# Softmax bookkeeping of a fused packed-attention and expert kernel: a 33rd column, two steps on GpSimd, a scale on the packed queries, a maximum with its sign turned

## The chip, the cores and the metric

One core of a Trainium2 chip. The metric is device time in microseconds (us) of one execution, as the median of three runs. The engines are TensorE (PE, its weight loads PEld), VectorE (DVE), ScalarE (ACT), GpSimd (POOL) and SyncE (SP, which issues most of the DMAs). Each engine works through its own list of instructions in order.

## The reference

Two attentions in a row, then a layer of eight experts of which each row takes one.

```python
def sm_attn(qq, kk, vv):
    s = scale * np.matmul(qq, kk.transpose(0, 1, 3, 2))   # scale = 1/8
    s = s - np.max(s, axis=-1, keepdims=True)
    a = np.exp(s)
    a = a / (np.sum(a, axis=-1, keepdims=True) + 1e-09)
    return np.matmul(a, vv)
p_packed = sm_attn(p, k, v)          # 32 packed queries against 576 keys
out = sm_attn(q, p_packed, p_packed) # 576 queries against the 32 packed results
...
expert_idx = np.argmax(logits, axis=1)
...
ye = np.maximum(xe @ w1[e], 0.0) @ w2[e]
out[mask] = gate_w[mask, None] * ye
```

Batch 8, heads 8, 576 rows, head size 64; the expert layer has 4608 rows of 512, 8 experts and a hidden size of 1024.

## The kernel before

The first part of the kernel is the attention of eight batches b, the second the expert layer. The attention's steps are written out by hand in the string ORDER, in which each token is one step of one batch: `k`, `v`, `q` issue the loads on SP's queue; `a` and `c` (function `s1`, four heads each) make the scores of the packed queries, their maximum and their exponentials; `r`, `u` and `l` transpose these; `p` (`pv`) multiplies them with v; `b` and `w` (`bd`, `wgp`) lay out the packed result. `S` (`s2`) makes the second attention's scores of two tiles of 128 rows (one tile in the steps ending in 4), `T` (`t2`) transposes their exponentials on TensorE, `O` (`o2`) multiplies and copies out. `E` and `F` are the routing's steps on DVE, `G` the indirect gathers that POOL issues, `P` the layout of the gathered rows, `X` (`scale`) the common scale of all rows. From this program order a planner with costs of its own lays out one list for each engine, so steps that stand behind one another in the program can lie interleaved on an engine.

In `s1` DVE takes the maximum m over 576 scores (L549) and multiplies it by -0.125 (L550); ACT's exponential (L551) takes m as its bias and 0.125 as its scale, and its accumulator gives the sum. When both halves are done, DVE adds 1e-9 to the sums (L560) and takes the reciprocal (L561); `pv` multiplies the reciprocal with a mask (L603) and with the product (L604). The packed queries reach their padded tile by a POOL copy (L493), two per batch.

In `s2` DVE takes the maximum of 32 scores for each of 16 groups (L667), subtracts it (L669) into tile e, ACT takes the exponential in place (L670), DVE sums (L672), adds 1e-9 (L673) and takes the reciprocal (L674), and POOL (for b under VB = 6) or DVE multiplies e by it in place (L676). Tile e has three buffers, and is held from the subtraction to the transposes of `t2` (L685).

POOL also computes the low halves of q (L525, function `split`), on which SP's q loads two buffers later wait, the sums lg of the router's scores (L715, for b under LB = 7), and issues the gathers (L430). In the routing, `of_expert` and `below` share one buffer with the tag "pb", and `places` takes its products mv from a buffer of 1024 elements. In `scale`, DVE spreads the maxima on a diagonal dg (L763), and a matmul with ones (onef, L765) hands every partition all of them.

The expert layer then runs over two groups of row tiles and four chunks of the hidden size: `l1` (L850, L853) and `l2` (L889) on TensorE, and on DVE and ACT the split of each loaded weight tile into a high and a low half (L144, L145). None of its lines is part of the change.

Of the kernel before, what the change touches and what calls it, by code (L numbers as in the profile page):

```python
# [7 lines left out]
F16 = mybir.dt.float16  # L8
F32 = mybir.dt.float32
I32 = mybir.dt.int32  # L10
AF = mybir.ActivationFunctionType
ALU = mybir.AluOpType
AX = mybir.AxisListType
# [3 lines left out]
P = 128  # L17
B, H, S, D = 8, 8, 576, 64
NPACK = 32
# [4 lines left out]
DM = 512  # L24
# [59 lines left out]
def packed_attention_moe(ctx, tc, qT, q1, kT, v4, v1, pT, wg, w1, w2, const, out):  # L84
# [82 lines left out]
    lg = r.tile([P, NT, NE], F32, name="lg")  # L167
    ppm = r.tile([P, B, 2], F32, name="ppm")
    sms = r.tile([P, B, 2], F32, name="sms")
    onef = r.tile([P, P], F32, name="onef")  # L170
    G.memset(onef, 1.0)
    quarter = r.tile([P, 4], F32, name="quarter")
    G.memset(quarter, 0.0)
# [16 lines left out]
    W = 9  # L190
# [108 lines left out]
    def places(k, nt, sf, pool, tag, room=None):  # L299

        a, z = parts[k]
        n = z - a
        inv = pool.tile([P, 4, n], F32, tag=tag, name=f"inv{a}")
        for t0 in range(0, nt, W):
            w = slice(t0, t0 + W)
            if k == 1:
                both = room(t0 // W).bitcast(F16)[:, 0 : 5 * W * n]
                ohs = both[:, 0 : W * n].rearrange("p (w n) -> p w n", n=n)
                mv = both[:, W * n :].rearrange("p (w c n) -> p w c n", c=4, n=n)
            else:  # L310
                ohs = room.tile([P, W, n], F16, tag="ohs", name="ohs", bufs=1)
                mv = room.tile([P, 2 * DM], F16, tag="mv", name="mv", bufs=1)[:, 0 : W * 4 * n]
                mv = mv.rearrange("p (w c n) -> p w c n", c=4, n=n)
            V.tensor_tensor(ohs, bc(cc["number"][:, a:z], [P, W, n], 1), bc(sf[:, w], [P, W, n], 2), op=ALU.is_equal)
            (G if k == 1 and t0 // W in MVG else V).tensor_tensor(
                mv, bc(ohs, [P, W, 4, n], 2), bc(coef[:, w, :], [P, W, 4, n], 3), op=ALU.mult
            )
            if k == 2:
                spread(t0, room)
            yield  # L320
            for t in range(t0, t0 + W):
                T.matmul(inv, ohr[t0][:, t - t0, :], mv[:, t - t0], start=(t == 0), stop=(t == nt - 1))
            yield
        tf = r.tile([P, n], F32, tag="tf", name=f"tf{a}")
        tz = r.tile([P, n], F32, tag="tz", name=f"tz{a}")
        pg = r.tile([P, n], F32, name=f"pg{a}")
        V.tensor_copy(tf, inv[:, 0, :])
        V.scalar_tensor_tensor(tf, inv[:, 1, :], -1.0, tf, op0=ALU.add, op1=ALU.add)
        V.tensor_scalar(gats[k], tf, 0.0, None, op0=ALU.max)
        V.tensor_scalar(tz, tf, 0.0, float(OOB), op0=ALU.is_lt, op1=ALU.mult)  # L330
        V.tensor_tensor(scas[k], tf, tz, op=ALU.add)
        V.tensor_copy(pg, inv[:, 2, :])
        V.tensor_tensor(pg, inv[:, 3, :], pg, op=ALU.add)
        pgs[k] = pg
        yield
# [130 lines left out]
    with ExitStack() as actx:  # L466
# [10 lines left out]
        bds = [one.tile([P, 2, 264], F32, name=f"bd{i}") for i in range(3)]  # L477
        pbs = [one.tile([P, NP, 2 * NPACK], F32, name=f"pb{i}") for i in range(2)]
        aLs = [one.tile([P, 2, P], F32, name=f"aL{i}") for i in range(2)]
        for t in pbs + aLs:  # L480
            G.memset(t, 0.0)

        loaded = {}
        lastld = [None]

        def load_k(b):
            k_s = ld.tile([P, NP, S], F32, tag="k", name=f"k{b}")
            p_s = pbs[b % 2]
            p_r = ld.tile([P, NP, NPACK], F32, tag="p", name=f"p{b}")
            nc.sync.dma_start(p_r, pT[b])  # L490
            for i in range(2):
                r = slice(D * i, D * i + D)
                G.tensor_copy(p_s[r, :, NPACK * i : NPACK * i + NPACK], p_r[r])  # L493
            if b == 0:
                nc.sync.dma_start(k_s[:, 0:2], kT[b][:, 0:2])
                nc.sync.dma_start(k_s[:, 2:4], kT[b][:, 2:4])
            else:
                nc.sync.dma_start(k_s, kT[b])
            loaded[b] = {"k": k_s, "p": p_s}
# [30 lines left out]
        def s1(b, g):  # L530

            k_s, p_s = loaded[b]["k"], loaded[b]["p"]
            if g == 0:

                a = wk.tile([P, 2 * S], F32, tag="a", name=f"a{b}")
                st[b] = {"a": a}
            a, sm = st[b]["a"], sms[:, b, :]
            ps = ps1.tile([P, 2, 512], F32, tag="s1", name="s1")
            for i in range(2):
                for j in range(2):  # L540
                    T.matmul(  # L541
                        ps[64 * j : 64 * j + 64, i, 0:288],
                        p_s[:, 2 * g + j, :],
                        k_s[:, 2 * g + j, 288 * i : 288 * i + 288],
                        start=True,
                        stop=True,
                    )
            m = wk.tile([P, 1], F32, tag="m1", name="m1")
            V.tensor_reduce(m, ps[:, :, 0:288], axis=AX.XY, op=ALU.max)  # L549
            V.tensor_scalar(m, m, -0.125, None, op0=ALU.mult)  # L550
            A.activation(  # L551
                a[:, S * g : S * g + S].rearrange("p (i s) -> p i s", s=288),
                ps[:, :, 0:288],
                AF.Exp,
                bias=m,
                scale=0.125,
                accum_out=sm[:, g : g + 1],
            )
            if g == 1:
                V.tensor_scalar(sm, sm, 1e-9, None, op0=ALU.add)  # L560
                V.reciprocal(sm, sm)  # L561

        def tr(b, g):
# [73 lines left out]
        def s2(b, i):  # L637

            ps = psq.tile([P, 512], F32, tag="s2", name="s2")
            if i < 4:  # L640
                hh = 2 * H
                for n in range(2):
                    for pr in range(NP):
                        for k, (x, y) in enumerate(PRODUCTS):
                            T.matmul(
                                ps[:, 256 * n + 64 * pr : 256 * n + 64 * pr + 64],
                                loaded[b]["q"][i // 2][x][:, pr, P * n : P * n + P],
                                ppTs[b % 3][:, y, pr, :],
                                start=(k == 0),
                                stop=(k == 2),  # L650
                            )
            else:
                hh = H
                for pr in range(NP):
                    for k, (x, y) in enumerate(PRODUCTS):
                        for n in range(2):
                            T.matmul(
                                ps[64 * n : 64 * n + 64, 64 * pr : 64 * pr + 64],
                                loaded[b - 1 + n]["r"][x][:, pr, :],
                                ppTs[(b - 1 + n) % 3][:, y, pr, :],  # L660
                                start=(k == 0),
                                stop=(k == 2),
                            )
                ps = ps[:, 0:256]
            p3 = ps.rearrange("p (h n) -> p h n", n=NPACK)
            m = wk.tile([P, 2 * H], F32, tag="m2", name="m2")[:, 0:hh]
            V.tensor_reduce(m, p3, axis=AX.X, op=ALU.max)  # L667
            e = wk.tile([P, 2 * H, NPACK], F32, tag="e2", name="e2", bufs=3)[:, 0:hh, :]
            V.tensor_tensor(e, p3, m.unsqueeze(2).to_broadcast([P, hh, NPACK]), op=ALU.subtract)  # L669
            last["A"] = A.activation(e, e, AF.Exp, scale=0.125 / SP)  # L670
            sm = wk.tile([P, 2 * H], F32, tag="sm2", name="sm2")[:, 0:hh]
            last["V"] = V.tensor_reduce(sm, e, axis=AX.X, op=ALU.add)  # L672
            V.tensor_scalar(sm, sm, 1e-9, None, op0=ALU.add)  # L673
            V.reciprocal(sm, sm)  # L674
            n, eng = ("V", V) if b >= VB else ("G", G)
            last[n] = eng.tensor_tensor(e, e, sm.unsqueeze(2).to_broadcast([P, hh, NPACK]), op=ALU.mult)  # L676
            return e

        def t2(e):
# [75 lines left out]
        def scale():  # L755

            xm = r.tile([P, 1], F32, name="xm")
            xa = r.tile([P, 1], F32, name="xa")
            V.tensor_tensor(ppm, ppm, sms, op=ALU.mult)
            V.tensor_reduce(xm, ppm, axis=AX.XY, op=ALU.max)  # L760

            dg = r.tile([P, P], F32, name="dg")
            V.tensor_scalar(dg, ident, xm, None, op0=ALU.mult)  # L763
            ps = pst.tile([P, P], F32, tag="tr", name="xmax")
            T.matmul(ps, onef, dg, start=True, stop=True)  # L765
            V.tensor_reduce(xa, ps, axis=AX.X, op=ALU.max)
            pow2(xa, xup, xdn)

# [331 lines left out]
```

## Time and profile before

| | |
|---|---|
| three runs | 618.74, 619.62, 625.78 us; median 619.62 us |
| the profiled execution | 621.44 us, of which its instructions span 619.5 us |
| PE busy | 536.5 us (87% of the span) |
| DVE busy | 469.3 us (76%) |
| ACT busy | 340.7 us (55%) |
| POOL busy | 220.5 us (36%) |

Busy time is the time in which an engine had at least one instruction under way, waits of the instruction for a resource within the engine included. A line such as L673 is a line of the kernel's source. In a row of the timeline the columns are the start, the duration, the engine, line and operation, the tiles written and read, the count, and in brackets the idle time of the engine before it with what ended it. A q behind an engine's name marks its queue: instructions that issue DMAs.

### The profile page before, as it was taken

To read this page: it belongs to the slowest core of one execution; us is meant where nothing else is said; L and a number is where in the kernel's file an instruction comes from. 1 tells how busy PE (TensorE), PEld (TensorE's weight loads), DVE (VectorE), ACT (ScalarE), POOL (GpSimd) and SP (SyncE) were. 2 spreads that over 40 slices of the span, in tenths; PEclk is the share of its full clock that TensorE was granted. 3 is DMA by queue.
4 is the path that set the end of the run, shared out by engine and by line. 5 is a ranking of instruction groups with operands and counts; after the bars stand their busy time and mean duration, and the time that the engine had idled before them with its cause. 6 is when DMAs were issued, how large, how long until landed. Compare 5 with 4: busy or idle time off the path is not lost. (4 is left out here: it accounts for less than half of the span.)

```text
span 619.5 us, 13722 instructions
## 1 busy us (share of the span) xinstructions
PE 536.5 (87%) x4227; PEld 314.3 (51%) x4227; DVE 469.3 (76%) x981; ACT 340.7 (55%) x688; POOL 220.5 (36%) x254
## 2 busy tenths in 40 slices
PE   3899986786768999989999967998999899999990
PEld 1667665565535645634554533455456445445440
DVE  1478995875867998999799849566548988998850
ACT  2568694564447886652772535135877527627400
POOL 2466663521836400330230568662102102201471
PEclk9799997897879999999999998999999999999996
DMA  8987958268748984897697699999859958967751
GB/s 321 397 277 272 394 175 292 85 192 300 245 181 242 245 218 154 180 243 249 158 264 243 182 176 297 281 231 217 191 168 245 274 174 196 273 229 169 138 223 55
DMA packets 132344, 140.13 MB, mean 226 GB/s; under 512 B 96623, under 2 KB 109039, under 8 KB 130352
## 3 DMA queue, kind: packets, MB, share of 16 engines
q1 hardware_dynamic: 116560, 110.62, 66.1%
q0 software_dynamic: 5920, 19.14, 9.8%
q10 hardware_dynamic: 9792, 9.44, 4.5%
q8 instruction: 42, 0.69, 0.5%
q14 instruction: 30, 0.25, 0.1%
HBM read 97.49 MB, written 19.14 MB: 188 GB/s over the span
## 5 line engine op out<-in xcount | busy, mean ns | idle before, releaser
L850 PE MATMUL psa<-w1r,x 128*128 (+1 forms) x656 | 197.0, 383 | 12.0 <-ACT x L713 5.6
L889 PE MATMUL py<-w2r,h 128*128 (+1 forms) x984 | 194.7, 379 | 10.3 <-ACT w2r L144 5.3
L853 PE MATMUL psa<-w1r,x 128*128 (+1 forms) x656 | 163.1, 275 | 0.2 <-DVE x L459 0.2
L863 POOL TENSOR_TENSOR hs<-u,hs 128x256 f16<-128x256 f32 x76 | 66.9, 882 | 243.9 <-DVE hs L862 228.5
L889 PEld LDWEIGHTS <-h 128*128 128x128 f16 (+1 forms) x984 | 87.8, 100 | 114.5 <-issue 13.1
L850 PEld LDWEIGHTS <-x 128*128 128x128 f16 (+1 forms) x656 | 59.7, 101 | 74.7 <-issue 6.3
L898 DVE SCALAR_TENSOR_TENSOR y<-py,gpl,y 128x512 f32<-128x512 f32 x111 | 79.4, 741 | 11.0 <-PE py L889 10.5
L145 DVE SCALAR_TENSOR_TENSOR w2r<-stage,w2r 128x1024 f16<-128x1024 f32 x56 | 74.4, 1328 | 12.4 <-ACT w2r L144 12.2
L855 ACT ACTIVATE u<-psa 128x256 f32<-128x256 f32 x148 | 53.2, 375 | 54.8 <-PE psa L853 44.7
L145 DVE SCALAR_TENSOR_TENSOR w1r<-stage,w1r 128x1024 f16<-128x1024 f32 x56 | 68.1, 1217 | 11.1 <-ACT w1r L144 11.1
L144 ACT ACTIVATE w1r<-stage 128x1024 f16<-128x1024 f32 x56 | 58.0, 1051 | 29.3 <-DMA stage<-w 28.2
L853 PEld LDWEIGHTS <-x 128*128 128x128 f16 (+1 forms) x656 | 59.7, 101 | 15.1 <-issue 7.9
L856 DVE SCALAR_TENSOR_TENSOR u<-psa,u 128x256 f32<-128x256 f32 x148 | 57.7, 413 | 11.7 <-ACT u L855 11.5
L144 ACT ACTIVATE w2r<-stage 128x1024 f16<-128x1024 f32 x56 | 58.5, 1045 | 0.0
L525 POOL TENSOR_TENSOR ql<-q,qh 128x1024 f16<-128x1024 f32 x16 | 34.3, 2143 | 35.2 <-ACT qh L524 34.4
L709 PE MATMUL x<-bd,a2T 128*128 128x264 f32 x128 | 42.2, 457 | 2.6 <-ACT a2T L687 2.4
L900 POOL DMA_INDIRECT out_rows<-y,sca x37 | 37.0, 1000 | 14.4 <-DVE y L898 7.4
L861 ACT ACTIVATE u<-u 128x256 f32<-128x256 f32 x76 | 31.2, 410 | 15.2 <-DVE u L856 14.7
L865 ACT ACTIVATE hs<-u 128x256 f16<-128x256 f32 x72 | 29.6, 412 | 16.4 <-DVE u L856 16.4
L866 DVE SCALAR_TENSOR_TENSOR hs<-u,hs 128x256 f16<-128x256 f32 x72 | 35.2, 490 | 4.4 <-ACT hs L865 4.4
L430 POOL DMA_INDIRECT g<-xd,gat x18 | 23.8, 1323 | 28.3 <-PE psa L853 24.8
L541 PE MATMUL s<-k,pb 128*64 128x288 f32 x128 | 21.9, 468 | 11.4 <-ACT a L551 6.0
(188 smaller groups left out, 680.2 us busy)
## 6 DMA issues: line engine op xcount, KB each, us to landing
stage<-w SPq DMA_DIRECT2D x112, 512.0 KB, 4.6
v<-v SPq DMA_DIRECT2D x8, 1024.0 KB, 8.3
q<-qT SPq DMA_DIRECT2D x16, 512.0 KB, 5.8
k<-kT SPq DMA_DIRECT2D x7, 1152.0 KB, 8.7
xd<-x ACTq DMA_DIRECT2D x22, 256.0 KB, 3.5
xd<-w2r ACTq DMA_DIRECT2D x14, 256.0 KB, 4.2
h<-hs SPq DMA_TRANSPOSE x76, 4.5
k<-kT SPq DMA_DIRECT2D x2, 576.0 KB
```

The lines of the kernel that those rows point to most:

```text
L144: A.activation(hi, src, AF.Copy, scale=SW)
L145: V.scalar_tensor_tensor(lo, src, SW, hi, op0=ALU.mult, op1=ALU.subtract)
L709: T.matmul(ps, aT[:, 2 * n + g, :], bds[b % 3][:, g, :], start=True, stop=True)
L850: T.matmul(ps[c], x[:, 0, k, c], w, start=(k == 0), stop=False, **kw)
L853: last["T"] = T.matmul(ps[c, 0:FC], x[:, 1, k, c], w, start=False, stop=(k == 3), **kw)
L855: A.activation(u, ps[:, FC:], AF.Copy, scale=SH)
L856: V.scalar_tensor_tensor(u, ps[:, 0:FC], SH, u, op0=ALU.mult, op1=ALU.add)
L863: last["G"] = G.tensor_tensor(hs[:, 1], u, hs[:, 0], op=ALU.subtract)
L866: last["V"] = V.scalar_tensor_tensor(hs[:, 1], u, 0.0, hs[:, 0], op0=ALU.max, op1=ALU.subtract)
L889: last["T"] = T.matmul(ps[c], h[:, hp, f, c], w, start=(n == 0), stop=(n == 5), **kw)
L898: last["V"] = V.scalar_tensor_tensor(y, ps, at(gpls, j), y, op0=ALU.mult, op1=ALU.add)
L900: i = G.indirect_dma_start(out, bass.IndirectOffsetOnAxis(ap=at(scas, j), axis=0), yt.pop(j), None, bounds_check=NT * P - 1, oob_is_err=False,
```

## The change

Four edits, and three that only make room in memory:

- `s2`: the exponentials go into one of two lasting tiles of 16 groups of 33 columns, whose 33rd column holds 1e-9 from the start. The sum runs over 33 columns, and DVE's addition L673 goes away. The multiplication by the reciprocal no longer works in place: it reads this tile and writes tile e, which now has two buffers in place of three.
- `s1`: the addition of 1e-9 to the two sums goes from DVE to POOL; DVE's reciprocal stays behind it.
- `load_k`: POOL's copy of the packed queries becomes a multiplication by 0.125.
- `s1`: the exponential no longer scales, and DVE's L550 goes away: the maximum is taken with its sign turned in the reduction itself.
- Memory: onef shrinks from 128 columns to one that the matmul in `scale` reads 128 times over, dg shares the tag "pb", and the first stage's mv shrinks to what it uses.

```diff
-    onef = r.tile([P, P], F32, name="onef")
+    onef = r.tile([P, 1], F32, name="onef")
...
-                mv = room.tile([P, 2 * DM], F16, tag="mv", name="mv", bufs=1)[:, 0 : W * 4 * n]
+                mv = room.tile([P, 2 * DM if k else W * 4 * n], F16, tag="mv", name="mv", bufs=1)[:, 0 : W * 4 * n]
...
+        e1s = [one.tile([P, 2 * H, NPACK + 1], F32, name=f"e1{i}") for i in range(2)]
+        ne = [0]
...
+        for t in e1s:
+            G.memset(t[:, :, NPACK : NPACK + 1], 1e-9)
...
-                G.tensor_copy(p_s[r, :, NPACK * i : NPACK * i + NPACK], p_r[r])
+                G.tensor_scalar(p_s[r, :, NPACK * i : NPACK * i + NPACK], p_r[r], 0.125, None, op0=ALU.mult)
...
-            V.tensor_reduce(m, ps[:, :, 0:288], axis=AX.XY, op=ALU.max)
-            V.tensor_scalar(m, m, -0.125, None, op0=ALU.mult)
+            V.tensor_reduce(m, ps[:, :, 0:288], axis=AX.XY, op=ALU.max, negate=True)
...
-                scale=0.125,
...
             if g == 1:
-                V.tensor_scalar(sm, sm, 1e-9, None, op0=ALU.add)
+                G.tensor_scalar(sm, sm, 1e-9, None, op0=ALU.add)
                 V.reciprocal(sm, sm)
...
-            e = wk.tile([P, 2 * H, NPACK], F32, tag="e2", name="e2", bufs=3)[:, 0:hh, :]
-            V.tensor_tensor(e, p3, m.unsqueeze(2).to_broadcast([P, hh, NPACK]), op=ALU.subtract)
-            last["A"] = A.activation(e, e, AF.Exp, scale=0.125 / SP)
+            e1 = e1s[ne[0] % 2][:, 0:hh, :]
+            ne[0] += 1
+            V.tensor_tensor(e1[:, :, 0:NPACK], p3, m.unsqueeze(2).to_broadcast([P, hh, NPACK]), op=ALU.subtract)
+            last["A"] = A.activation(e1[:, :, 0:NPACK], e1[:, :, 0:NPACK], AF.Exp, scale=0.125 / SP)
...
-            last["V"] = V.tensor_reduce(sm, e, axis=AX.X, op=ALU.add)
-            V.tensor_scalar(sm, sm, 1e-9, None, op0=ALU.add)
+            last["V"] = V.tensor_reduce(sm, e1, axis=AX.X, op=ALU.add)
             V.reciprocal(sm, sm)
             n, eng = ("V", V) if b >= VB else ("G", G)
-            last[n] = eng.tensor_tensor(e, e, sm.unsqueeze(2).to_broadcast([P, hh, NPACK]), op=ALU.mult)
+            e = wk.tile([P, 2 * H, NPACK], F32, tag="e2", name="e2", bufs=2)[:, 0:hh, :]
+            last[n] = eng.tensor_tensor(
+                e, e1[:, :, 0:NPACK], sm.unsqueeze(2).to_broadcast([P, hh, NPACK]), op=ALU.mult
+            )
             return e
...
-            dg = r.tile([P, P], F32, name="dg")
+            dg = r.tile([P, P], F32, tag="pb", name="dg")
...
-            T.matmul(ps, onef, dg, start=True, stop=True)
+            T.matmul(ps, onef.to_broadcast([P, P]), dg, start=True, stop=True)
```

## Rows read from the trace of the kernel before

**Rows 1.** Busy time by stretch: microseconds, engines PE to POOL, TensorE clock, DMA share, GB/s

```profile
0.00:28.00 28.00, 15.70 (x162) 10.13 (x162) 6.89 (x22) 9.12 (x18) 9.40 (x29) 0.88 0.95 358
28.00:96.00 68.00, 62.91 (x1003) 46.33 (x1002) 59.48 (x140) 51.61 (x115) 42.91 (x51) 0.98 0.76 278
96.00:134.00 38.00, 28.66 (x431) 22.20 (x430) 26.17 (x94) 19.15 (x43) 13.37 (x19) 0.86 0.50 174
134.00:182.00 48.00, 31.50 (x248) 22.34 (x242) 31.34 (x119) 21.06 (x46) 17.60 (x19) 0.82 0.78 259
182.00:606.00 424.00, 397.78 (x2393) 213.27 (x2393) 345.40 (x609) 239.79 (x468) 135.58 (x138) 0.99 0.86 216
```

**Rows 2.** Groups by line, 0 to 310 us: busy us, mean ns, idle before

```profile
L672 DVE TENSOR_REDUCE sm<-e 128x16 f32<-128x512 f32 (+1 forms) x20 | 12.3, 620 | 3.2 <-ACT e L670 3.1
L673 DVE TENSOR_SCALAR sm<-sm 128x16 f32<-128x16 f32 (+1 forms) x20 | 6.4, 324 | 0.1
L560 DVE TENSOR_SCALAR sms<-sms 128x2 f32<-128x2 f32 x8 | 4.8, 596 | 2.7 <-ACT a L551 2.7
L493 POOL COPY pb<-p 64x128 f32<-64x128 f32 x16 | 4.6, 289 | 8.1 <-DMA p<-pT 7.6
...
L715 POOL TENSOR_TENSOR lg<-w2r 128x8 f32<-128x8 f32 x14 | 2.8, 205 | 7.5 <-ACT w2r L713 7.5
L550 DVE TENSOR_SCALAR m<-m 128x1 f32<-128x1 f32 x16 | 2.3, 146 | 0.2
```

**Rows 3.** DVE's busy time in L673 alone, by stretch

```profile
28.00:96.00 68.00, 4.93 (x12) 0.98 0.76 278
96.00:134.00 38.00, 0.81 (x5) 0.86 0.50 174
134.00:182.00 48.00, 0.62 (x3) 0.82 0.78 259
```

**Rows 4.** DVE's busy time in L560 alone

```profile
28.00:96.00 68.00, 4.27 (x5) 0.98 0.76 278
```

**Rows 5.** DVE's busy time in L550 alone

```profile
28.00:96.00 68.00, 1.58 (x11) 0.98 0.76 278
```

**Rows 6.** Timeline, one pack's sums beside POOL's split of q

```profile
35.59 2.13 POOL L525 TENSOR_TENSOR ql<-q,qh 128x1024 f16<-128x1024 f32 x1 [1.05 <-ACT qh L524]
...
36.55 1.20 DVE L560 TENSOR_SCALAR sms<-sms 128x2 f32<-128x2 f32 x1 [0.30 <-ACT a L551]
...
37.67 1.05 POOL L676 TENSOR_TENSOR e<-e,sm 128x512 f32<-128x512 f32 x1
...
37.78 0.17 DVE L561 RECIPROCAL sms<-sms 128x2 f32<-128x2 f32 x1
```

**Rows 7.** Timeline, a sum of s2 beside POOL's split, and POOL beside DVE

```profile
91.23 2.33 POOL L525 TENSOR_TENSOR ql<-q,qh 128x1024 f16<-128x1024 f32 x1 [1.60 <-ACT qh L524]
...
91.48 2.11 DVE L673 TENSOR_SCALAR sm<-sm 128x16 f32<-128x16 f32 x1
...
93.62 0.25 DVE L674 RECIPROCAL sm<-sm 128x16 f32<-128x16 f32 x1
...
95.01 1.21 DVE L145 SCALAR_TENSOR_TENSOR w1r<-stage,w1r 128x1024 f16<-128x1024 f32 x1
95.02 1.72 POOL L525 TENSOR_TENSOR rl<-r,rh 128x256 f16<-128x256 f32 x1
```

**Rows 8.** Timeline, POOL's products of s2 and DVE's next subtraction but one

```profile
80.92 1.62 POOL L676 TENSOR_TENSOR e<-e,sm 128x512 f32<-128x512 f32 x2 [0.18 <-DVE sm L674]
...
81.48 0.69 DVE L669 TENSOR_TENSOR e<-s,m 128x512 f32<-128x512 f32 x1
```

**Rows 9.** Timeline, the attention's two long stalls on ACT and TensorE

```profile
104.13 0.38 ACT L623 ACTIVATE ppT<-bd 128x256 f16<-128x256 f32 x1 [4.11 <-DMA v<-v]
...
172.85 0.38 ACT L713 COPY x<-x 128x264 f32<-128x264 f32 x1 [6.88 <-POOL lg L715]
...
174.89 0.59 PE L850 MATMUL psa<-w1r,x 128*128 x1 [5.57 <-ACT x L713]
```

## The prediction, made before the change was run

> **What bounds the kernel now.** I first cut the span by stages with the view of busy time by stretch [rows 1]. From 182 us on the expert layer holds TensorE: 397.78 of 424 us busy at a granted clock of 0.99. No line of the change lies there. What the change can move is the time at which that stage begins. Ahead of it stand four stretches. Up to 28 us the transfers set the pace (DMA share 0.95, DVE busy for 6.89 us). From 28 to 96 us two engines are nearly full: TensorE with 62.91 of 68 us, DVE with 59.48. From 96 to 182 us none is full (TensorE 60.2 of 86, DVE 57.5): the attention's last batches run as a chain of short steps, with stalls such as the 4.11 us in which ACT waits for the load of v, and the 6.88 us in which it waits for POOL's sums of the router's scores behind the gathers, after which TensorE's first expert tile comes 5.57 us late [rows 9].
>
> Second, I asked what DVE's 59.48 us are made of. L673 adds a constant to 16 numbers in each partition; over all stretches it has a mean of 324 ns, L560 (two numbers) one of 596 ns, while L550 (one number) takes 146 ns [rows 2]. The timeline says why. L560 at 36.55 us lasts 1.20 us and ends 0.03 us behind POOL's split of q; L673 at 91.48 us lasts 2.11 us and ends 0.03 us behind another one [rows 6, 7]. These instructions are held by POOL, and the hold counts as busy. It goes the other way too: POOL's split of 256 columns took 1.72 us beside DVE's L145 [rows 7]. Undisturbed, L673 takes some 0.16 us (0.81 us for five from 96 to 134 us [rows 3]), so its 12 in this stretch are 4.93 us, of which 12 x 0.16 = 1.9 us is their own work and 3.0 us hold; L560's five are 4.27 us, some 3.4 us of it hold [rows 4]; three of the five look like the one in [rows 6].
>
> The Trainium skill's page SBUF — State Buffer, section "Who interferes with whom", says that DVE's copies and tensor_scalar in a two-port mode, and DVE instructions with two SBUF inputs, take a pair of ports that GpSimd also needs, whoever comes first holding it for the whole instruction. The two timelines agree [rows 6, 7]. By the same rule the addition moved to POOL would be held whenever one of DVE's two-input instructions runs.
>
> **The change part by part.** I sum against the profiled execution, 621.44 us (span 619.5 us).
>
> *L673 goes, 20 times.* Between 28 and 96 us that is 4.93 us of DVE's time [rows 3]. Against it each sum runs over 528 in place of 512 numbers, 16/512 of 620 ns = 19 ns, or 0.4 us for all 20 [rows 2]. A hold isn't wholly gained: if DVE's next two-input instruction falls into the same split, it is held in its place. I take 3.5 us. From 96 to 182 us the eight others are 1.43 us [rows 3], in a chain where a step saved may count or may only lengthen another wait: 0 to 1.4 us, I take 0.5.
>
> *L550 goes, 16 times.* Eleven lie between 28 and 96 us, 1.58 us [rows 5]; starts of neighbouring short instructions lie closer than their durations, so I take 1.0. It also shortens the way from the scores to the exponential by some 0.15 us in each `s1`; up to 28 us that is covered by transfers, and I take 0.3 there. The turned sign within the reduction is not in the trace; its nearest row without one is the same reduction, and I take no cost, with 16 x 0.15 = 2.3 us as the other end, which would cancel this part.
>
> *L560 moves to POOL, 8 times.* DVE loses 4.27 us between 28 and 96 us [rows 4], but L561 now waits for POOL, and behind L561 on DVE stand L603 and the next maxima. Where POOL is idle the addition costs what its smallest arithmetic costs, 0.2 us (128x8, L715 [rows 2]). Where a split runs, the addition waits for its end, just as the held L560 did: in [rows 6] it could start at 37.72 us, and L561 comes at about 38.0 us in place of 37.78, or past 38.9 us if POOL's product of 1.05 us goes first. DVE gains only if the planner put other work ahead of L561. On POOL the addition waits in order for ACT's accumulator, and behind it stand the split of q, on which SP's next q load waits, and the products on which TensorE's transposes wait; POOL has 25 us of idle time in the 68 [rows 1]. Ends: a gain of 4.3 us, a loss of 8 (next part). I take a gain of 0.5.
>
> The Trainium skill's page GPSIMD Engine Reference, section "Engine selection", advises VectorE and not GpSimd for elementwise work on a tile. Here the nearest rows differ by 0.04 us (0.205 us against L673's undisturbed 0.16), so by size alone it changes nothing; the wait does.
>
> *Buffers.* Before, a subtraction needed the transposes of three steps earlier; now it needs the product of two steps earlier, and the product needs the transposes of two steps earlier. I went through ORDER for each step: the closest case is the subtraction at 81.48 us, which needs the product of two steps before, ended by about 82.0 us in [rows 8]. That is a wait of 0.5 us for DVE, less the 0.2 us by which that product can come earlier without L673. In all other steps the older product or transpose has ended in time. Cost 0.3 us.
>
> *The packed queries' scale.* POOL's 16 copies of 289 ns become multiplications of the same size [rows 2]. They lie right behind their load and a batch or more ahead of their use; if a multiplication took twice as long it would be 4.6 us of POOL's time, hidden by its idle time. Cost nothing; uncovered only for the first batch, 0.3 us at most. The memory edits and the ones read as a broadcast touch one matmul, and dg is read before anything else takes its buffer, since DVE itself waits for that matmul: nothing.
>
> *The sum.* DVE gains 3.5 + 1.0 + 0.5 - 0.3 - 0.2 (12 longer sums) = 4.5 us between 28 and 96 us. TensorE has only 68 - 62.91 = 5.1 us of idle time there [rows 1], so even if DVE alone caused all of it, no more than about that can come out. With 0.3 us before and 0.5 us behind, 5.3 us; of it I count 5, since the later stalls for transfers partly swallow it. The expert layer shifts as a whole. 621.44 - 5 = 616.4 us for the profiled execution; the median of the runs lies 1.8 us under it, so 614.6, and I say 615.
>
> **The rivals.**
>
> *It is swallowed* (about 619.5 us). TensorE's 62.91 us of 68 speak for it: if its weight loads and matmuls were the true limit, DVE's time would turn into waiting. So does the 4.11 us stall behind v's load [rows 9]. Against it speaks that v's load is itself issued when a product of the attention frees its buffer, so it would move along.
>
> *Slower: L561 blocks DVE* (about 624 us). In the three packs where L560 is long today, POOL has a split of 2.13 us under way and a smaller split (a quarter of its columns, so some 0.5 us) or a product (1.05 us) behind it [rows 6]. If the planner puts the addition behind all of these, it ends up to 2.13 + 0.5 + 1.05 + 0.2 = 3.9 us behind the accumulator, against some 1.3 us today (4.27 us less two undisturbed ones, by three): 2.6 us more in three packs, 7.8 us, and with the five others 8 us. Less the 4 us that L673 and L550 give, 4 us more than now: 619.62 + 4 = 624. From the point at which DVE's new waits at L561 exceed about 4.5 us, the change loses. Against it: a planner that sees POOL's queue can set L561 later.
>
> *More than the sum* (about 607 us). All that goes from DVE is 6.4 + 4.8 + 2.3 = 13.5 us [rows 2]; if all of it counted, 619.62 - 13.5 = 606. A smaller piece with the same result would be another order on POOL near 170 us, which takes away part of the 6.88 us stall [rows 9]. TensorE's small idle time between 28 and 96 us speaks against the first, and nothing in the change aims at the second, though the planner lays all lists out anew.
>
> *The change doesn't do what it says:* the new tile's rows of 33 columns could be slower to write or read for ACT, DVE or POOL. The trace has no such form; 20 steps with 0.1 us each on four instructions would be 8 us of engine time, partly hidden, and this ends near the swallowed case.
>
> **How the numbers follow.** Forecast 615 us (611 to 618): chance 0.44. Swallowed, the slow rows of 33 with it: 0.23. Slower: 0.18. More: 0.15. Two per cent, about what a measurement of this kernel can tell from no change (its three runs lie 7 us apart), is 12.4 us: 607.2 and 632.0. Half of the case "more" lies under the first; of "slower" a quarter over the second, with two or three stalls of the kind of [rows 9] added. So 0.09 faster, 0.05 slower, 0.86 within. For 8 in 10 I leave out the lower half of "more" and the upper part of "slower": 605 to 627 us.
>
> **What would show it.** Right: DVE's sum of the attention shorter by some 10 us of busy time, no DVE instruction of two numbers held for over a microsecond, TensorE's L850 of [rows 9] some 5 us earlier than 174.89 us, the rest shifted. Wrong: DVE idle ahead of L561 with POOL as the releaser, above 4 us in total; a first expert tile at the same time or later; a reduction L549 that takes longer than before; or an expert layer that itself got longer or shorter, which no step here explains.

## The result, and the profile after

The changed kernel takes 618.51 us (median of 20 runs), the kernel before 624.71 us in 20 runs beside it: a ratio of 0.9872, with a 95% interval of 0.9834 to 0.991. The medians lie 6.2 us apart; the ratio, which leaves out the runs more than 1.5% above the fastest of their kernel (ten of the changed kernel's 20), makes it 8 us (624.71 times 0.0128), or 1.3%, and within the two per cent of the prediction. The profiles show less, spans of 619.5 and 619.8 us before and 614.9 us now: both of before are of executions (621.44 and 621.7 us) some 3 us under its median. The first profile of the changed kernel fell on an execution of 621.07 us, slower than its median; the rows below are from a second one, of 616.92 us.

Busy time by stretch of the changed kernel, the stretches of [rows 1] (columns: PE, PEld, DVE, ACT, POOL, TensorE's granted clock, DMA share, GB/s):

```profile
0.00:28.00 28.00, 19.22 (x286) 12.20 (x286) 9.07 (x23) 12.40 (x24) 13.45 (x34) 1.00 0.94 364
28.00:96.00 68.00, 62.23 (x899) 45.65 (x898) 51.24 (x112) 49.63 (x115) 46.04 (x59) 0.96 0.79 292
96.00:134.00 38.00, 30.01 (x429) 23.65 (x429) 29.22 (x90) 20.80 (x44) 13.33 (x20) 0.81 0.60 207
134.00:182.00 48.00, 35.22 (x282) 24.61 (x281) 37.65 (x126) 26.10 (x57) 26.53 (x24) 0.92 0.81 270
182.00:606.00 424.00, 391.32 (x2333) 209.60 (x2333) 338.05 (x588) 232.22 (x450) 125.26 (x131) 0.97 0.86 210
```

Two things stand out against [rows 1]. DVE is 8.2 us less busy between 28 and 96 us. And the first stretch, in which I had expected 0.3 us, holds 286 matmuls in place of 162: the attention gets ahead before 28 us. From 134 to 182 us all engines do more, since the expert layer begins sooner.

Groups of the same kernel by line, from 0 to 310 us (busy us, mean ns, idle before), which answer to [rows 2]:

```profile
L676 DVE TENSOR_REDUCE sm<-e 128x16 f32<-128x528 f32 (+1 forms) x20 | 12.7, 635 | 0.3 <-ACT e L674 0.3
...
L554 DVE TENSOR_REDUCE m<-s 128x1 f32<-128x576 f32 x16 | 12.0, 752 | 11.9 <-PE s L546 11.6 <-PE wgp L635 0.3
...
L498 POOL TENSOR_SCALAR pb<-p 64x128 f32<-64x128 f32 x16 | 8.4, 528 | 10.9 <-DMA p<-pT 7.7 <-PE s L546 2.6
...
L606 DVE TENSOR_TENSOR ms<-sms,quarter 128x8 f32<-128x8 f32 x8 | 5.0, 623 | 0.2
...
L563 POOL TENSOR_SCALAR sms<-sms 128x2 f32<-128x2 f32 x8 | 1.7, 214 | 5.2 <-ACT a L555 3.8 <-ACT sh L234 1.1
...
L564 DVE RECIPROCAL sms<-sms 128x2 f32<-128x2 f32 x8 | 1.3, 163 | 5.1 <-POOL sms L563 5.1
```

The sum over 33 columns costs 15 ns more, against the 19 forecast, and the reduction with its sign turned 752 ns, as without (751 ns). POOL's addition takes 214 ns. The reciprocal now waits 5.1 us in all for it: over 4 us of this the prediction had named as a sign of its being wrong, and the time fell all the same. L606, the product behind it, has a mean of 623 ns where its undisturbed time is 166 ns: two of its eight are held, by 1.8 us each. Before, three were held, by 0.6 to 0.8 us:

```profile
L603 DVE TENSOR_TENSOR ms<-sms,quarter 128x8 f32<-128x8 f32 x8 | 3.3, 413 | 0.3
```

One of the two:

```profile
41.37 0.21 POOL L563 TENSOR_SCALAR sms<-sms 128x2 f32<-128x2 f32 x1
...
41.61 0.17 DVE L564 RECIPROCAL sms<-sms 128x2 f32<-128x2 f32 x1 [0.89 <-POOL sms L563]
...
41.66 2.13 POOL L530 TENSOR_TENSOR ql<-q,qh 128x1024 f16<-128x1024 f32 x1
41.81 2.00 DVE L606 TENSOR_TENSOR ms<-sms,quarter 128x8 f32<-128x8 f32 x1
```

In this timeline of the changed kernel POOL's next split begins 0.05 us behind the reciprocal, and the next DVE instruction with two inputs is held for 1.8 us. So a hold taken from L560 can pass on to its neighbour. In sum a part of it does: L606 is busy for 1.7 us more than L603 was, and the 4.8 us of L560 are gone from DVE.

### The profile page after: what moved, and what is told of

Same layout as the page of the kernel before. It is cut to its first block, busy times and chain, and to the rows that moved or that the text cites. A ratio compares the mean times of both kernels' runs of the same rounds, so it can differ in the third digit from the quotient of the medians.

```text
span 618.9 us, 13689 instructions
## 1 busy us (share of the span) xinstructions
PE 539.1 (87%) x4227; PEld 314.8 (51%) x4227; DVE 464.4 (75%) x937; ACT 341.7 (55%) x688; POOL 225.5 (36%) x264
## 4 chain that ended last, share of the span: by engine, by line
PE 42%; DMA 6%; DVE 5%; ACT 3%; issue 2%; POOL 0%; POOLq 0%; ACTq 0%; DVEq 0%
PE py L895 27%; PE psa L856 10%; PE psa L859 5%; DMA stage<-w 3%; DVE w2r L145 2%; ACT w2r L144 2%; DMA g<-xd,gat 2%; DMA x<-xs 2%; DVE u L862 1%; DVE hs L872 1%; ACT hs L871 0%; ACT u L867 0%; DVE xs L449 0%; DVE hs L868 0%; ACT u L861 0%
## 5 line engine op out<-in xcount | busy, mean ns | idle before, releaser
L895 PE MATMUL py<-w2r,h 128*128 (+1 forms) x984 | 198.7, 384 | 17.8 <-ACT w2r L144 14.4
L145 DVE SCALAR_TENSOR_TENSOR w2r<-stage,w2r 128x1024 f16<-128x1024 f32 x56 | 74.8, 1336 | 12.1 <-ACT w2r L144 11.9
L145 DVE SCALAR_TENSOR_TENSOR w1r<-stage,w1r 128x1024 f16<-128x1024 f32 x56 | 68.8, 1228 | 11.6 <-ACT w1r L144 11.6
L144 ACT ACTIVATE w1r<-stage 128x1024 f16<-128x1024 f32 x56 | 58.1, 1052 | 28.8 <-DMA stage<-w 26.8
L862 DVE SCALAR_TENSOR_TENSOR u<-psa,u 128x256 f32<-128x256 f32 x148 | 57.9, 413 | 13.6 <-ACT u L861 13.4
L530 POOL TENSOR_TENSOR ql<-q,qh 128x1024 f16<-128x1024 f32 x16 | 35.1, 2196 | 14.8 <-ACT qh L529 11.7
L872 DVE SCALAR_TENSOR_TENSOR hs<-u,hs 128x256 f16<-128x256 f32 x72 | 36.6, 508 | 4.3 <-ACT hs L871 4.0
L430 POOL DMA_INDIRECT g<-xd,gat x18 | 22.4, 1245 | 28.3 <-PE psa L859 24.2
L546 PE MATMUL s<-k,pb 128*64 128x288 f32 x128 | 22.4, 465 | 11.5 <-ACT a L555 6.2
```

Of the source, the lines that this page charges most:

```text
L144: A.activation(hi, src, AF.Copy, scale=SW)
L145: V.scalar_tensor_tensor(lo, src, SW, hi, op0=ALU.mult, op1=ALU.subtract)
L862: V.scalar_tensor_tensor(u, ps[:, 0:FC], SH, u, op0=ALU.mult, op1=ALU.add)
L872: last["V"] = V.scalar_tensor_tensor(hs[:, 1], u, 0.0, hs[:, 0], op0=ALU.max, op1=ALU.subtract)
L895: last["T"] = T.matmul(ps[c], h[:, hp, f, c], w, start=(n == 0), stop=(n == 5), **kw)
```

## The experiments

All were timed in five rounds beside the kernel before. For each I read when certain steps begin: the product of the second and of the sixth batch (DVE's reduction behind `pv`), the first gather on POOL, and the first `l2` product on TensorE, with the span of the same profile. The expectations number their theories: 1, the work and the holds that DVE lost are the gain; 2, the lists as the planner newly laid them out; 3, the move of L560 alone; 4, L550's place between the maximum and the exponential of `s1`. The runs were spread over three chips, on which the kernel before had medians from 622.63 to 627.83 us: times are compared as ratios, and a span is that of one execution.

| kernel | 2nd batch | 6th batch | first gather | first l2 | span | ratio (interval) |
|---|---|---|---|---|---|---|
| before | 31.6 | 96.3 | 154.2 | 214.5 | 619.5 | |
| before again | 31.8 | 96.5 | 151.3 | 211.2 | 619.8 | 1.004 (1.000 to 1.008) |
| changed, again | 27.3 | 92.8 | 146.6 | 206.0 | 614.9 | 0.987 (0.981 to 0.993) |
| column alone | 31.8 | 91.3 | 147.5 | 206.5 | 611.2 | 0.989 (0.984 to 0.994) |
| maximum's sign alone | 26.4 | 90.6 | 151.7 | 211.7 | 617.7 | 0.992 (0.988 to 0.996) |
| POOL's addition alone | 32.5 | 96.9 | 150.6 | 210.7 | 619.1 | 0.988 (0.979 to 0.997) |
| changed without maximum | 34.0 | 94.0 | 145.3 | 206.3 | 613.8 | 0.991 (0.985 to 0.996) |
| changed without column | 26.9 | 89.8 | 148.1 | 207.3 | 624.6 | 0.986 (0.972 to 1.001) |
| changed without POOL's addition | 28.8 | 92.3 | 148.3 | 206.2 | 617.8 | 0.996 (0.992 to 1.001) |
| no additions at all | 27.2 | 90.9 | 147.7 | 207.2 | 620.2 | 0.989 (0.980 to 0.999) |
| L673 back, as scalar | 27.2 | 91.4 | 140.4 | 199.4 | 606.3 | 0.977 (0.973 to 0.982) |
| L673 back, as reduction | 26.5 | 90.8 | 143.3 | 204.4 | 614.0 | 0.992 (0.987 to 0.997) |
| before, a multiplication more | 31.6 | 102.0 | 156.8 | 217.3 | 624.1 | 1.013 (1.007 to 1.020) |

**The changed kernel again.** No edit.

> The changed kernel once more, for a second profile. All theories: 0.987 of the kernel before, as measured (0.983 to 0.991). Theory 1 (what DVE lost was real work and holds, so the attention ends earlier): the last product of the first attention (matmuls pv) ends about 8 us before 133.9 us, the last copy of the second one about 12 us before 174.5 us, as in the first profile. Theory 2 (the planner's new lists removed single stalls by chance): the same times, but the gain sits in one or two places, the stall of 4.1 us behind v's load and that of 6.9 us behind the gathers. Open besides: the wait of 10.9 us that TensorE had near 380 us in the first profile. If it belongs to the changed kernel it comes again; if it is a matter of one execution it is some 3 us, as in the kernel before.

Measured: 0.9874. The steps come within 2 us of the first profile's, and the long wait of TensorE near 380 us came again (8.6 us after 10.9 us, below), so it belongs to this kernel.

**The kernel before again.** No edit.

> The kernel before, unchanged, as a second profile of it and as the measure of what a ratio means here. All theories: ratio 1.000 (0.995 to 1.005), the holds of DVE behind POOL in the same places as in its first profile (some 12 us of them between 28 and 96 us), the last copy of the second attention near 174.5 us, the first l2 product near 214.5 us.

Measured: 1.004, with an interval that just takes in 1. The holds lie in the same places, and the lists of the engines are the same, instruction by instruction. Between two profiles of one program the first gather differs by 2.9 us: less than that is read from no row of the table behind the sixth batch.

**Each part alone.** The column:

```diff
+            e1 = e1s[ne[0] % 2][:, 0:hh, :]
...
-            V.tensor_scalar(sm, sm, 1e-9, None, op0=ALU.add)
```

> The kernel before with the 33rd column alone (two lasting tiles of 33 columns, product not in place, L673 gone, the memory edits); L550 and L560 stay on DVE. Theory 1: this is the largest part, 4 to 5 us faster, ratio 0.992 to 0.994. Theory 2 (plan and stalls): no order can be told, anything from 0.98 to 1.01. Theory 3 (the move of L560 to POOL is the gain, since it held DVE for 3.4 us): nothing, 0.999 to 1.001.

The maximum:

```diff
-            V.tensor_reduce(m, ps[:, :, 0:288], axis=AX.XY, op=ALU.max)
-            V.tensor_scalar(m, m, -0.125, None, op0=ALU.mult)
+            V.tensor_reduce(m, ps[:, :, 0:288], axis=AX.XY, op=ALU.max, negate=True)
```

> The kernel before with the scale on the packed queries and the sign turned in the reduction alone: L550 gone, POOL's copies are multiplications. Theory 1: 1 to 1.5 us faster, ratio 0.998. The reduction with the turned sign takes the same 0.75 us. POOL's multiplication showed 0.53 us against the copy's 0.29 in the changed kernel; hidden by POOL's idle time. If that were not hidden: up to 3 us slower, 1.005.

POOL's addition:

```diff
-                V.tensor_scalar(sm, sm, 1e-9, None, op0=ALU.add)
+                G.tensor_scalar(sm, sm, 1e-9, None, op0=ALU.add)
```

> The kernel before with only the addition L560 moved to POOL. Theory 1: 0 to 1 us faster, ratio 0.998 to 1.000, since the addition waits for the same split of q as the held instruction did. Theory 3: 3 to 8 us faster, 0.987 to 0.995. The rival of the prediction (DVE's reciprocal blocked): 4 to 8 us slower, 1.006 to 1.013, with DVE idle ahead of the reciprocal and POOL as the releaser.

Measured: 0.9893, 0.9919 and 0.9882. Each part alone gives about two thirds of the whole or more; together they give hardly more than one. No theory that adds terms foretold that. The table shows that they get there by different ways. Against the first profile of before, the sign alone is 5.2 us ahead at the second batch and 5.7 us at the sixth, and then loses it (2.5 us ahead at the first gather, and 0.4 us behind the second profile's). The column alone is level at the second batch and 5.0 us ahead at the sixth. POOL's addition alone is 0.4 to 0.9 us behind both profiles at these two, and behind them all its steps and its span come within 0.7 us of the second profile of before. So the move itself shows no gain in the trace, and nothing there answers to its ratio of 0.988, whose interval reaches 0.997. In it the rival of the prediction can be seen at work once:

```profile
61.52 2.13 POOL L525 TENSOR_TENSOR ql<-q,qh 128x1024 f16<-128x1024 f32 x1
63.60 1.05 POOL L676 TENSOR_TENSOR e<-e,sm 128x512 f32<-128x512 f32 x1
64.61 0.67 POOL L525 TENSOR_TENSOR rl<-r,rh 128x256 f16<-128x256 f32 x1
65.36 0.21 POOL L560 TENSOR_SCALAR sms<-sms 128x2 f32<-128x2 f32 x1
```

```profile
65.61 0.17 DVE L561 RECIPROCAL sms<-sms 128x2 f32<-128x2 f32 x1 [1.42 <-POOL sms L560]
```

The addition stood behind a split, a product and a smaller split, as priced, and DVE waited 1.42 us; in the other places it did not stand so far back (5.5 us of such waits in all).

**Each part taken out of the changed kernel.** Edits: the lines above, turned back one part at a time.

> The changed kernel without the scale on the packed queries and the turned sign (L550 back on DVE, POOL copies): column and POOL's addition alone. Theory 4, formed from the runs so far: L550 stands between the maximum and the exponential of s1, whose scores have one PSUM buffer, so the way from one s1 to the next passes through it and through whatever DVE has in front of it; with the turned sign the exponential starts 0.03 us behind the maximum, without it 0.8 to 1.5 us behind in the first four steps. Then the second batch's product (ppm, L600 of before) comes near 31.7 us, as in the kernel before, and not near 27.3 us as in the changed one, and the whole is 2 to 5 us slower than the changed kernel, ratio 0.991 to 0.995. Theory 2 (only the lists as a whole matter): product near either, ratio anywhere from 0.975 to 1.01.

> The changed kernel without the 33rd column: turned sign and POOL's addition alone; L673 on DVE, three buffers of e, product in place. Theory 4: second batch's product near 27.3 us; ratio 0.985 to 0.992. Theory 1 (L673 is the largest part): half of the gain or less is left, 0.994 to 0.997, with L673 held for 1 to 2 us in some places. Theory 2: no telling.

> The changed kernel with L560's addition back on DVE: column and turned sign alone. Theory 4: second batch's product near 27.3 us, ratio 0.983 to 0.990, and no wait of DVE's reciprocal for POOL (1.99 us at 95.8 us in the changed kernel). If the addition on POOL is a gain of its own: 2 to 4 us slower than the changed kernel, 0.991 to 0.994. If that wait costs: 1 to 3 us faster, 0.982 to 0.985.

Measured: 0.9906, 0.9864 (with an interval up to 1.001) and 0.996. The second batch obeys theory 4 in every kernel of the table: with the sign turned in the reduction it comes at 26.4 to 28.8 us, with L550 in place at 31.6 to 34.0 us. The total does not: without the column the ratio is no worse, and without POOL's addition it is worse, though the 1.99 us wait is gone; its interval, 0.992 to 1.001, touches that of the changed kernel's second timing (0.981 to 0.993).

**L673 back on DVE.** First as it was, then a reduction over one column in its place.

```diff
-            last["V"] = V.tensor_reduce(sm, e1, axis=AX.X, op=ALU.add)
+            last["V"] = V.tensor_reduce(sm, e1[:, :, 0:NPACK], axis=AX.X, op=ALU.add)
+            V.tensor_scalar(sm, sm, 1e-9, None, op0=ALU.add)
```

> The changed kernel with L673's addition put back on DVE (sum over 32 columns, then the addition as a tensor_scalar on the 16 sums); the new tiles, the move to POOL and the sign stay. Theory 1: 3 to 5 us slower than the changed kernel, ratio to the kernel before 0.993 to 0.996; some of these 20 instructions are held for 1 to 2 us. Theory 2: no telling order, about 0.99. If the buffers of the changed kernel are the gain: 0.987, no loss.

```diff
-            last["V"] = V.tensor_reduce(sm, e1, axis=AX.X, op=ALU.add)
+            last["V"] = V.tensor_reduce(sn, e1, axis=AX.X, op=ALU.add)
+            V.tensor_reduce(sm, sn.unsqueeze(2), axis=AX.X, op=ALU.add)
```

> As the run before, but in the addition's place stands a reduction over one column on DVE (20 of them, each copying the 16 sums): the same count of DVE instructions in the same place, of a kind whose instances never lasted longer in the trace of before (sums over 32 columns, maxima and reciprocals show no such spread). Theory 1, with the hold as the main part: 1 to 2 us slower than the changed kernel, ratio 0.989 to 0.991, 2 to 3 us better than with the tensor_scalar. If the instruction's own work or place in the chain is the price: as the run before.

Measured: 0.9773 and 0.9921. With 20 instructions more, one of them held for 1.6 us, the first is the fastest kernel of the study (607.6 us, median), 1% under the changed one. Its interval, 0.973 to 0.982, is clear of that of the changed kernel's 20 runs and just touches that of its second timing. The second, whose added reductions are held nowhere (0.28 us at most), is slower than the first by 1.5%, the reverse of what was expected.

```profile
L677 DVE TENSOR_SCALAR sm<-sm 128x16 f32<-128x16 f32 (+1 forms) x20 | 5.6, 282 | 0.1
```

```profile
102.14 1.76 DVE L677 TENSOR_SCALAR sm<-sm 128x16 f32<-128x16 f32 x1
```

So the time that L673 takes, holds included, is not what the total follows; theory 1 falls here. Twelve of the 20 additions lie ahead of the sixth batch, which comes at 91.4 us with them and at 92.8 us without.

**A second multiplication in the kernel before.**

```diff
-            V.tensor_scalar(m, m, -0.125, None, op0=ALU.mult)
+            V.tensor_scalar(m, m, -0.25, None, op0=ALU.mult)
+            V.tensor_scalar(m, m, 0.5, None, op0=ALU.mult)
```

> The kernel before with one DVE instruction more in each s1: the factor -0.125 is put on in two steps, -0.25 and 0.5. It adds work and lets the planner lay out its lists anew. Theory 1 (work taken from DVE is the gain): 1 to 2.5 us slower, ratio 1.002 to 1.004. Theory 2 (the lists of the kernel before happen to be poor, so that any edit that lays them out anew gains): faster, 0.988 to 0.996, with fewer holds than 12 us between 28 and 96 us though DVE has more to do.

Measured: 1.0134, some 8 us slower for 2.3 us of DVE's work. Not any new layout gains, then, so theory 2 in its plain form falls too. DVE's busy time between 28 and 96 us fell to 48.09 us in it, from 59.48, and the kernel is the slowest: that number says little of how far the attention has come.

**No additions.** The kernel before with the turned sign, and both lines that add 1e-9 left out.

> The kernel before with the turned sign, and with both additions of 1e-9 left out (a sum of exponentials that holds the maximum's own is at least 1, where 1e-9 is under half a unit of float32); e in place with three buffers, no 33rd column, nothing moved to POOL. Least work of all versions. Theory 1 and theory 4: as fast as the changed kernel or faster, 0.980 to 0.988. Theory 2 (lists): anywhere from 0.975 to 1.0, not ordered by work. A version that beats both kernels, if theory 4 holds and the waits for POOL and the holds are what is left.

Measured: 0.9892. The version with the least work is not the fastest.

## Why the prediction was right, and which of its terms were not

**The whole.** Forecast were 5 us less; 5 (spans of the second profiles), 6 (medians) and 8 (ratio) were measured, and the attention ends sooner and the expert layer shifts, as named. The 618.51 us themselves lie just above the 611 to 618 us of this case, because the kernel before, counted from 619.62 us, came out at 624.71 us. In all 14 profiles, the changed kernel's first one included, the first `l2` product comes 58 to 61 us behind the first gather, and the span ends 405 to 417 us behind that product. This last length differs by 3.6 us between the two profiles of the kernel before and by 5.9 us between those of the changed one, so no part of it is put down to the change.

The place of the gain is not the one forecast. Of the 5.3 us, 4.5 were to come between 28 and 96 us and 0.3 ahead of them. The changed kernel is 4.3 us ahead of the kernel before at the second batch and 3.5 us at the sixth: it has its lead by about 30 us, and nothing is added up to the sixth batch. That the sum came out right is in good part luck: one of its terms was mis-sized by some 4 us, and its largest one isn't seen.

For the kernel before, for the changed one and for the version with L673 back, TensorE's products with the second weights (last figures: first and last start):

```profile
L889 PE MATMUL py<-w2r,h x984: 376/379/631, 211.2 to 605.2; 128*128 x159, 128*64 128x512 f16 x38
```

```profile
L895 PE MATMUL py<-w2r,h x984: 376/379/631, 206.0 to 599.9; 128*128 x159, 128*64 128x512 f16 x38
```

```profile
L896 PE MATMUL py<-w2r,h x984: 376/379/632, 199.4 to 591.4; 128*128 x159, 128*64 128x512 f16 x38
```

**L673 (3.5 us, the largest term): not borne out.** With it back, the sixth batch came no later and the kernel was the fastest. The column alone does gain 5.0 us by the sixth batch, but as the version with L673 back is as far by then (91.4 us), that gain isn't shown to be L673's. My own caution, that a hold passes on to the next instruction with two inputs, is what the trace shows once (L606 above). It goes both ways: here, in the changed kernel, DVE's L145 is held by POOL's product until 91.75 us, and POOL's next split then takes 3.11 us:

```profile
90.70 1.05 POOL L680 TENSOR_TENSOR e<-e,sm 128x512 f32<-128x512 f32 x1 [2.75 <-ACT w1r L144]
...
91.01 1.82 DVE L145 SCALAR_TENSOR_TENSOR w1r<-stage,w1r 128x1024 f16<-128x1024 f32 x1
...
91.71 3.11 POOL L530 TENSOR_TENSOR ql<-q,qh 128x1024 f16<-128x1024 f32 x1
```

**L550 (1.3 us with the first stretch): mis-sized, and its cover misread.** I wrote that transfers cover the first 28 us. But the scores of `s1` have one PSUM buffer, so its steps stand in a chain: matmul, maximum, L550, exponential, next matmul. ACT's rows in the second profile of before and in the changed kernel:

```profile
8.96 1.28 ACT L551 ACT_TABLE_LOAD   x1 [8.96 <-DVE m L550]
10.26 0.74 ACT L551 ACTIVATE a<-s,m 128x576 f32<-128x576 f32 x1
```

```profile
0.73 1.28 ACT L555 ACT_TABLE_LOAD   x1 [0.73 <-PEq L1085]
8.88 0.74 ACT L555 ACTIVATE a<-s,m 128x576 f32<-128x576 f32 x1 [6.87 <-DVE m L554]
```

The third step, in the same two profiles:

```profile
18.19 0.76 DVE L549 TENSOR_REDUCE m<-s 128x1 f32<-128x576 f32 x1 [1.25 <-PE s L541]
19.83 0.50 DVE L748 SCALAR_TENSOR_TENSOR wgp<-wgs,wgp 128x32 f16<-128x32 f32 x1 [0.89 <-ACT wgp L747]
20.25 0.14 DVE L550 TENSOR_SCALAR m<-m 128x1 f32<-128x1 f32 x1
```

```profile
20.49 0.74 ACT L551 ACTIVATE a<-s,m 128x576 f32<-128x576 f32 x1 [0.69 <-DVE m L550]
```

```profile
18.16 0.76 DVE L554 TENSOR_REDUCE m<-s 128x1 f32<-128x576 f32 x1 [2.84 <-PE s L546]
```

```profile
18.95 0.74 ACT L555 ACTIVATE a<-s,m 128x576 f32<-128x576 f32 x1 [0.36 <-DVE m L554]
```

From the end of the maximum to the start of the exponential the first four steps took 1.56, 0.76, 1.54 and 1.41 us before, 5.3 us in all; with the turned sign they take 0.03 or 0.04 us each. 1.3 us of it is the load of ACT's table, which waited with the first exponential and now runs at the start. The rest is the multiplication itself, and what stands between: in the second and the fourth step a copy that ACT has ahead of the exponential, in the third a DVE instruction that waits for ACT. That answers to the 3 to 5 us by which the kernels with this part are ahead of the kernel before at the second batch, against the 0.3 us forecast. In the whole this part alone gave 0.8%.

**L560 (0.5 us): no gain is seen.** The addition waits for the same splits as L560 did. Before, L560 and L603 were busy for 4.8 and 3.3 us and DVE stood 2.7 us ahead of L560, 10.8 us in all; now it is 5.0 us for L606 and 5.1 us of waiting for POOL, 10.1 us: 0.7 us less, close to the forecast. But in all three pairs of kernels that differ by this move alone, the one with it comes later at the sixth batch: 96.9 against 96.3 us, 94.0 against 91.3 and 92.8 against 92.3.

**POOL's scale: "the same size" fails, and no cost of it is seen.** It takes 528 ns against the copy's 289, close to the bound of twice that I gave.

**The later stalls.** Of the 4.1 us behind v's load [rows 9], half is a matter of the execution: the second profile of before has 2.1 us, with the load issued no sooner (95.05 us after 94.55 us).

```profile
102.28 0.38 ACT L623 ACTIVATE ppT<-bd 128x256 f16<-128x256 f32 x1 [2.08 <-DMA v<-v]
```

In the changed kernel, which issues the load at 89.81 us, the wait is gone; with POOL's addition alone it is 1.3 us. The 6.88 us behind POOL's sums shrank to 2.5 us, as the rival "more than the sum" had it, and TensorE's tile behind them comes at 163.88 us, 8 to 11 us sooner than before and not 5:

```profile
163.45 0.38 ACT L719 COPY x<-x 128x264 f32<-128x264 f32 x1 [2.47 <-POOL lg L721]
```

```profile
163.88 0.38 PE L856 MATMUL psa<-w1r,x 128*128 x1 [0.94 <-ACT x L719]
```

Yet from the first gather to the first `l2` product it is 59.4 us there and 60.3 us before, so little of this reaches the total. A stall new to me lies in the expert layer's change of row groups. TensorE's waits from 340 to 410 us in the changed kernel, then in the second profile of before (line, releaser: us in total, times, longest):

```profile
PE py L895 <- ACT w2r L144: 8.6, 1, 8.6
PE psx L456 <- DMA g<-xd,gat: 7.0, 1, 7.0
```

```profile
PE psx L456 <- DMA g<-xd,gat: 7.8, 1, 7.8
PE py L889 <- DMA h<-hs: 5.7, 1, 5.7
```

These are 15.6 against 13.5 us (11.5 in its first profile), and 11.7 us in the version with L673 back. From the first `l2` product to the end, though, the changed kernel takes 408.9 us and the kernel before 408.6 (405.0 in its first profile), so that they give back some of the gain is not shown.

**What stays open.** Between the sixth batch's product and the first gather lie 49.0 us in the fastest version, 51.3 to 61.1 us in the others, with no order by the work that they do. The layout of the lists is not the whole reason. The kernel before and its copy have the same lists, and 57.9 and 54.8 us. The column alone and the changed kernel without the maximum differ in the eight additions, on DVE or POOL, and in a few neighbours of them on DVE, all ahead of 100 us; TensorE's, ACT's and SP's lists are the same throughout. They take 56.2 and 51.3 us, and part on TensorE: the second is 0.5 us behind at 106 us and 2.6 us ahead at the next maximum of `s2` near 120 us. In between, busy time of both from 112 to 120 us (columns as above):

```profile
112.00:120.00 8.00, 8.00 (x50) 5.97 (x51) 4.14 (x19) 2.96 (x7) 0.83 (x2) 0.50 0.10 33
```

```profile
112.00:120.00 8.00, 8.00 (x95) 6.57 (x95) 6.15 (x22) 4.54 (x11) 1.02 (x3) 0.80 0.19 65
```

TensorE has no idle time here in either; in the first it runs at a granted clock of 0.50, the lower of its two levels (1.2 and 2.4 GHz), in the second at the lower one for part of the stretch only (0.80). In the 8 us ahead it was busy for 3.90 and 4.39 us. Over the whole way the granted clock is 0.82 and 0.90 in these two, 0.86 in the fastest version and 0.80 in the one that takes 61.1 us (the sign alone). So the granted clock is a part of the scatter, which the prediction did not price; how the rest divides between clock, loads and lists is not shown. A single part's share of the 8 us can't be given; that L550's removal brings 3 to 5 us up to the second batch can.

## What to carry to other kernels

Where a step with a single buffer passes between engines, price an instruction removed from it by the whole gap that it opens, with what stands ahead of it on its engine and what its wait holds up, not by its own duration. An instruction that is slow because a neighbour engine holds it need not be a cost of its own: take it away, and the next one can be held. Where a planner lays out the lists anew, measure an unchanged copy and each part alone before the sum is believed, and compare the lists and the granted clock of two profiles before a difference is put down to an edit. Here three parts of 0.8 to 1.2% each made 1.3% together, and two profiles with the same lists lay 3 us apart in one stretch.

## What the runs showed of the hardware that was not expected

ACT's table load (1.28 us) began behind L550, at 8.96 us, in the second profile of before, and between 8.7 and 9.1 us in every kernel with L550; it began at 0.73 or 0.74 us in every kernel whose exponential takes its bias straight from the maximum. Why is not shown. POOL's multiplication of 64x128 by a constant took 528 ns where its copy took 289 ns. A DVE product of eight numbers in each partition lasted 2.00 us beside POOL's split, twelve times its undisturbed 166 ns. Two kernels with the same list on TensorE, which is busy all through 112 to 120 us in both, had a granted clock of 0.50 and 0.80 there.
